# An attention and mixer kernel on one core: q and k of the last four batches loaded in token order and turned by DMA transposes

## The chip, the core and the metric

The kernel runs on one NeuronCore of a Trainium2 chip. The core has a matmul engine (TensorE, PE; its weight loads are listed as PEld), a vector engine (VectorE, DVE), an activation engine (ScalarE, ACT), a general engine (GpSimd, POOL) and a synchronising engine (SyncE, SP). DMAs are issued from queues: here SP's and POOL's, and ACT's once at the start. They all move their data through the core's 16 DMA engines. The metric is the device time of one execution in microseconds.

## The reference

The reference computes causal attention in which 16 extra "beacon" keys and values stand ahead of each batch's own, and then a mixer in two steps.

```python
# q, k, v: [B=8, H=8, S=576, D=64]; beacon_k, beacon_v: [8, 8, 16, 64]
k_all = concatenate([beacon_k, k], axis=2);  v_all = concatenate([beacon_v, v], axis=2)
scores = q @ k_all.T / sqrt(D);  scores[causal] = -1e9       # beacons are seen by every query
x = softmax(scores) @ v_all                                   # to [8, 576, 512]
u = x + (x.T @ U @ V).T                                       # rank 32, over the 576 tokens
out = u + relu(u @ w_ch1) @ w_ch2                             # 512 -> 2048 -> 512, float32
```

## The kernel before, in words

The inputs are float32. All products run in float16 and add up in float32 in PSUM, which is handed out as eight banks in turn.

**Attention.** The work goes by pairs of heads: 8 batches with 4 pairs each, p = 0 to 31, with `b, c = divmod(p, 4)`. Scores are made with keys on partitions, so both q and k are needed with channels on partitions (`qT`, `kT`). For a pair, `regroup_of` (L483, the copy itself at L218, on DVE) reorders the loaded q and k into `pr`. `qkT_units` (L221) then turns them on PE, in one unit for q and one for k: one transpose of the first 80 rows (L227) and four of 128 columns (L229). DVE brings each result out of PSUM in two copies (L230, L231). `score_units` (L238) makes the scores (L257) in two visits, has ACT exponentiate them (L263), and DVE applies the masks (L244, L246). `av_unit` (L277) multiplies with v (L281) and divides by the sums (L289, L290) into `xb`. A pair's scores are made one pair ahead of its products with v, and its transposes two pairs ahead.

**Loads.** POOL's queue casts to float16 on the way. For q and k it makes pieces of four neighbouring tokens a partition and head (`main_load`, L167) and a small load of the first tokens (`head_load`, L161); beacons have their own (L164). v comes in token order, 128 tokens a tile, in five DMAs (L174). The tiles of q and k alternate between two buffers, and so do `kT` and v. Batch 0's q and k come in float32 through SP and ACT and are rounded on chip by ACT, DVE and POOL (`group_first`, L477).

**Mixer.** `mix_units` (L294) adds the low-rank term to a batch's x and stores it turned in `uT`. Its head is one unit, its parts are six. Where it is "turned", five DMA transposes on SP's queue (L301) bring x to `uT`, and DVE adds the term in place (L341). Otherwise PE transposes x (L325) and adds the term in PSUM, and ACT (L345) or DVE (L343) copies it out. `mlp_units` (L351) makes blocks of 512 rows: 16 units of the first product with a relu (g, L370, relu on ACT L374 or DVE L376) and 16 units of the second (c, L386). Each unit is four matmuls of 512 columns; every fourth c unit ends in an addition on DVE (L399) and an output store on SP (L404), from four buffers. A block begins with four DMA transposes on SP (L360).

**Order.** The order of all engines is written out by hand. Mixer and MLP units wait in a queue, and `fill` takes a number of them, the quota, between the parts of a pair's attention. `mix` (L546) is called for a batch when its last pair is done. It takes the turned form if the batch is 2 or later and the queue holds at least 17 units (`LAG + 5`), and then puts the head behind 12 of them. Batches 0 and 1 run with the counts in `FIRST`; then come 16 units, and seven more among the attention of the next pairs; from batch 2 on the quota applies. What is left in the queue runs at the end.

```python
turned = b >= NF and len(queue) >= LAG + 5                   # L548
quota = 8 if b == NF else 9 if c == 0 else 8                 # L655, NF = 2
```

Of the kernel before, what the change touches and what calls it, by code (L numbers as in the profile page):

```python
# [17 lines left out]
P = 128  # L18
# [9 lines left out]
def kernel(  # L28
# [57 lines left out]
    loads = ctx.enter_context(tc.tile_pool(name="loads", bufs=2))  # L86
# [96 lines left out]
    def qk_tiles():  # L183

        hd = [loads.tile([P, H, D], F16, name=f"hd{i}", tag=f"hd{i}") for i in range(2)]
        st = [stage.tile([P, H, 4 * D], F16, name=f"st{i}", tag=f"st{i}") for i in range(2)]
        return hd, st
# [9 lines left out]
    def emit_loads(b, L, vs):  # L197
        k_loads(b, L, ALLH)
        q_loads(b, L, ALLH)
        beacon_load(nc.gpsimd, beacon_k[b], L[0][0], ALLH)  # L200
        v_loads(v[b], beacon_v[b], vs, ALLH)
# [237 lines left out]
    def load_batch(b):  # L439
        Ls[b] = qk_tiles()  # L440
        emit_loads(b, Ls[b], vss[b % 2])
# [5 lines left out]
    def load_first():  # L447
# [4 lines left out]
        hd = [loads.tile([P, H, D], F16, name=f"hd{i}", tag=f"hd{i}") for i in range(2)]  # L452
        Ls[0] = hd, [main[:, i, :, :] for i in range(2)]
# [47 lines left out]
    def qkT_of(p):  # L501
        b, c = divmod(p, NH2)
        new_qT_of(p)
        return qkT_units(Ls[b], prs[p], qTs[b], kTs[b % 2], c)
# [15 lines left out]
    AHEAD = 16  # L520
    LAG = 12
# [3 lines left out]

    IDLE = [10, 3, 2, 2]
    queue = []
    state = {"t": 0}

# [32 lines left out]
    with tc.manual_schedule(engines={ENG.PE, ENG.Activation, ENG.DVE, ENG.SP, ENG.Pool}):  # L562
# [41 lines left out]
        for p in range(NP1):  # L604
# [8 lines left out]
            if p + 2 < NP1:  # L613
                if p == 0:
                    seq.append(lambda: group_first(2, 1, V))
                elif p == 1:
                    seq.insert(1, lambda: group_first(3, 1, act_copy))
                else:
                    seq.append(lambda p=p: regroup_of(p + 2))
                qk = [lambda i=i, p=p: qkT_of(p + 2)[i]() for i in range(2)]  # L620
            seq += av[0:1] + qk + av[1:2]
            if p + 2 < NP1:
                new_qT_of(p + 2)
                sc = scores_of(p + 2)
                seq.append(lambda sc=sc, p=p: sc[0](IDLE[3] if p < NH2 else 0))
# [16 lines left out]
        for p in range(NP1, NP):  # L642
            b, c = divmod(p, NH2)
            if c == 0 and b + 1 < B:
                load_batch(b + 1)
            sc = scores_of(p + 1) if p + 1 < NP else []
            qk = []
            if p + 2 < NP:
                regroup_of(p + 2)
                qk = qkT_of(p + 2)  # L650
            av = av_of(p)
# [3 lines left out]
            quota = 8 if b == NF else 9 if c == 0 else 8  # L655
# [112 lines left out]
```

## Time and profile before

| | before |
|---|---|
| median of 3 runs | 377.83 us (377.72 to 378.54) |
| profiled execution | 378.74 us, its span 377.1 us |
| busy PE, DVE, ACT, POOL | 360.0, 217.9, 170.3, 85.6 us |
| DMA | 100349 packets, 36.33 MB |
| POOL's queue (q0) | 65904 packets, 17.54 MB, 49.9% of 16 engines' span |
| SP's queue (q1) | 33952 packets, 17.90 MB, 19.8% |

In the profile's lines, L12 is line 12 of the kernel before. A group of instructions stands as `output<-inputs`, with tile sizes as partitions x elements. After the bar come the busy time in us, the mean of one in ns, and the time the engine was idle just ahead of these instructions, with what ended it. In a timeline a row has its start, its length in us (of all its instructions together), engine and line, and in brackets the idle time ahead of it. A "q" behind an engine's name is its queue of DMAs; the length there is that of issuing, not of moving the data. The DMA share of a stretch is the time of all packets over the time of 16 engines; packets overlap on an engine, so it can be over 1.

### The profile page before, as it was taken

To read this page: it belongs to the slowest core of one execution; us is meant where nothing else is said; L and a number is where in the kernel's file an instruction comes from. 1 tells how busy PE (TensorE), PEld (TensorE's weight loads), DVE (VectorE), ACT (ScalarE), POOL (GpSimd) and SP (SyncE) were. 2 spreads that over 40 slices of the span, in tenths; PEclk is the share of its full clock that TensorE was granted. 3 is DMA by queue.
4 is the path that set the end of the run, shared out by engine and by line. 5 is a ranking of instruction groups with operands and counts; after the bars stand their busy time and mean duration, and the time that the engine had idled before them with its cause. 6 is when DMAs were issued, how large, how long until landed. Compare 5 with 4: busy or idle time off the path is not lost.

```text
span 377.1 us, 7980 instructions
## 1 busy us (share of the span) xinstructions
PE 360.0 (95%) x3180; PEld 185.4 (49%) x3180; DVE 217.9 (58%) x602; ACT 170.3 (45%) x370; POOL 85.6 (23%) x126
## 2 busy tenths in 40 slices
PE   6768999999999999989999999989999999999995
PEld 2546455454555554544465545544554444444442
DVE  5868763465658666665666675785677352222311
ACT  3758662466435653466445663467441301401300
POOL 9998537302105302230323050000000000000000
PEclk9889999999999999999999999999999999999999
DMA  9999999944719951995199799133012402103111
GB/s 181 205 146 206 194 197 136 195 105 58 101 57 106 117 56 59 93 152 62 13 111 132 111 53 105 56 85 57 9 58 85 91 30 97 42 30 108 33 49 72
DMA packets 100349, 36.33 MB, mean 96 GB/s; under 512 B 76112, under 2 KB 94544, under 8 KB 100304
## 3 DMA queue, kind: packets, MB, share of 16 engines
q0 software_dynamic: 65904, 17.54, 49.9%
q1 hardware_dynamic: 33952, 17.90, 19.8%
q8 instruction: 27, 0.44, 0.5%
q10 hardware_dynamic: 448, 0.30, 0.3%
q14 instruction: 18, 0.15, 0.1%
HBM read 37.86 MB, written 9.44 MB: 125 GB/s over the span
## 4 chain that ended last, share of the span: by engine, by line
PE 89%; DVE 6%; ACT 2%; DMA 1%; SPq 1%; issue 1%; ACTq 0%
PE gps L370 34%; PE cps L386 33%; PE sps L257 7%; PE po L281 7%; PE tps L229 3%; PE ups L335 2%; ACT expt L263 1%; PE ups L325 1%; DMA stm<-in_q_dram 1%; DVE kT L231 1%; PE qtp L310 1%; DVE qT L231 1%; DVE xb L290 1%; PE tps L227 1%; DVE expt L244 1%
## 5 line engine op out<-in xcount | busy, mean ns | idle before, releaser
L263 ACT ACTIVATE expt<-sps 128x496 f16<-128x496 f32 (+2 forms) x256 | 111.2, 531 | 82.3 <-PE sps L257 82.3
L370 PE MATMUL gps<-uT,w 128*128 128x512 f16 x576 | 137.8, 379 | 1.2 <-ACT uT L345 1.2
L386 PE MATMUL cps<-w,gT 128*128 128x512 f16 x576 | 137.8, 379 | 0.0
L374 ACT ACTIVATE gT<-gps 128x512 f16<-128x512 f32 x86 | 51.5, 606 | 93.1 <-PE gps L370 91.9
L386 PEld LDWEIGHTS <-gT 128*128 128x128 f16 x576 | 52.4, 98 | 56.4 <-issue 4.4
L370 PEld LDWEIGHTS <-w 128*128 128x128 f16 x576 | 51.4, 97 | 57.2 <-issue 5.1
L376 DVE TENSOR_SCALAR gT<-gps 128x512 f16<-128x512 f32 x58 | 39.9, 690 | 41.4 <-PE gps L370 39.7
L399 DVE TENSOR_TENSOR ob<-cps,ut 128x512 f32<-128x512 f32 x32 | 22.1, 690 | 42.8 <-PE cps L386 42.2
L281 PEld LDWEIGHTS <-expt 128*128 128x128 f16 (+1 forms) x960 | 38.2, 99 | 12.4 <-DVE expt L246 0.7
L174 POOL DMA_DIRECT2D vs<-in_v_dram x50 | 40.1, 815 | 13.8 <-DMA w<-in_moe_w_ch_dram 6.0
L281 PE MATMUL po<-vs,expt 128*128 128x65 f16 (+1 forms) x960 | 40.8, 195 | 0.5 <-DVE expt L244 0.2
L257 PE MATMUL sps<-qT,kT 64*128 64x80 f16 (+4 forms) x384 | 34.3, 291 | 4.4 <-DVE kT L231 4.3
L244 DVE TENSOR_TENSOR expt<-expt,bigmask 128x512 f16<-128x512 f16 x64 | 27.0, 422 | 12.6 <-ACT expt L263 12.2
L290 DVE TENSOR_TENSOR xb<-po,rec 128x320 f16<-128x320 f32 x64 | 31.4, 491 | 2.2
L289 DVE RECIPROCAL rec<-po 128x5 f32<-128x5 f32 x64 | 12.0, 188 | 27.9 <-PE po L281 27.7
L257 PEld LDWEIGHTS <-kT 64*128 64x128 f16 x384 | 12.5, 96 | 31.2 <-issue 14.2
L229 PE MATMUL tps<-ident,pr 128*128 128x128 f16 x256 | 24.6, 222 | 0.5 <-DVE pr L218 0.5
L231 DVE COPY qT<-tps 128x512 f16<-128x512 f16 x32 | 21.8, 680 | 0.0
L231 DVE COPY kT<-tps 128x512 f16<-128x512 f16 x32 | 21.7, 678 | 0.0
L164 POOL DMA_DIRECT2D vs<-in_beacon_v_dram x10 | 5.3, 535 | 70.1 <-PE po L281 69.9
L229 PEld LDWEIGHTS <-pr 128*128 128x128 f16 x256 | 16.3, 99 | 6.2 <-DVE pr L218 0.8
L227 PE MATMUL tps<-ident,hd 80*128 80x80 f16 x64 | 13.1, 204 | 4.1 <-ACT hd L473 2.9
(65 smaller groups left out, 185.3 us busy)
## 6 DMA issues: line engine op xcount, KB each, us to landing
out_dram<-ob SPq DMA_DIRECT2D x36, 256.0 KB, 2.2
w<-in_moe_w_ch_dram POOLq DMA_DIRECT2D x4, 1024.0 KB, 11.5
st<-in_k_dram POOLq DMA_DIRECT2D x6, 512.0 KB, 6.9
st<-in_q_dram POOLq DMA_DIRECT2D x6, 512.0 KB, 7.5
vs<-in_v_dram POOLq DMA_DIRECT2D x18, 128.0 KB, 6.6
stm<-in_k_dram SPq DMA_DIRECT2D x4, 256.0 KB, 4.5
vs<-in_v_dram POOLq DMA_DIRECT2D x12, 64.0 KB, 6.5
stm<-in_q_dram SPq DMA_DIRECT2D x3, 256.0 KB, 5.9
```

The costliest lines, as they stand in the source:

```text
L174: nc.gpsimd.dma_start(out=dst[a : a + nq[j], j, :, :], in_=src[hs, ds(q0[j], nq[j]), :].rearrange("h p d -> p h d"))
L229: nc.tensor.transpose(ps[:, ds(NL + P * j, P)], pr[i][:, j, :, :], ident)
L231: nc.vector.tensor_copy(out=dst[:, c, w - 4 * P : w].rearrange("x (p j) -> x p j", j=4), in_=ps[:, NL:SK].rearrange("x (j p) -> x p j", j=4),)
L244: nc.vector.tensor_tensor(out=e4, in0=e4, in1=bigmask, op=ALU.min)
L257: nc.tensor.matmul(ps[g, i][:, ds(o, w)], kT[hp, c, ds(P * ch, P)], qT[hp, c, ds(qa, w)], start=True, stop=True,)
L263: nc.scalar.activation(out=ex[i][:, ds(SLOT * g, gw[g])], in_=ps[g, i][:, 0 : gw[g]], func=AF.Exp, scale=scale)
L281: nc.tensor.matmul(po[:, j, :], ex[0 : nk[c], ds(blk[(c, j)], P)], vs[0 : nk[c], ds(c * H * E + h * E, E)], start=(c == 0), stop=(c == j),)
L290: nc.vector.tensor_tensor(out=xb[:, :, ds(h * D, D)], in0=po[:, :, 0:D], in1=r.broadcast_to([P, NT, D]), op=ALU.mult)
L370: nc.tensor.matmul(g[:, 0:n], w1[:, cc, ts(dc, P)], uT[:, cc, ds(t0, n)], start=(cc == 0), stop=(cc == NCC - 1))
L374: nc.scalar.activation(out=gT["t"][:, dc, 0:n], in_=g[:, 0:n], func=AF.Relu)
L376: nc.vector.tensor_scalar_max(out=gT["t"][:, dc, 0:n], in0=g[:, 0:n], scalar1=0.0)
L386: nc.tensor.matmul(ps[:m, :], gT["t"][:, dc, ds(P * i, m)], w2[:, dc, :], start=(dc == 0), stop=turned and dc == NDC - 1, skip_group_check ...
```

## The change

It has four parts.

1. For batches 4 to 7 (`DT0 = 4`) q and k are loaded in token order: five DMAs each for q and k, 128 tokens a tile as v has them, and one for the beacons (`load_whole`). They are issued at the third pair of the batch two before. v's loads stay where they were.
2. Those tiles are turned by ten DMA transposes a batch on SP's queue (`turns`), straight into `kT` and `qT`: four ahead of each of the first two pairs of the batch before, and two ahead of the third. `regroup_of` and `qkT_of` are no longer called for pairs of batches 4 to 7.
3. The rounding of the last q set of batch 0 (`group_first(3, 1, act_copy)`) moves from the second pair, behind its exponentials, to the end of the first pair, ahead of the next scores.
4. The quota is 4 in batch 2 and 9 in all later pairs.

The tiles for the first tokens (`hd`) now lie in the same tile as the others (`st`), so both come free together.

```diff
-    loads = ctx.enter_context(tc.tile_pool(name="loads", bufs=2))
...
     def qk_tiles():
-        hd = [loads.tile([P, H, D], F16, name=f"hd{i}", tag=f"hd{i}") for i in range(2)]
-        st = [stage.tile([P, H, 4 * D], F16, name=f"st{i}", tag=f"st{i}") for i in range(2)]
-        return hd, st
+        t = [stage.tile([P, NT * DM], F16, name=f"st{i}", tag=f"st{i}") for i in range(2)]
+        st = [x[:, 0 : 4 * DM].rearrange("p (h e) -> p h e", h=H) for x in t]
+        hd = [x[:, 4 * DM :].rearrange("p (h d) -> p h d", h=H) for x in t]
+        whole = [x[:, :].rearrange("p (j h d) -> p j h d", h=H, d=D) for x in t]
+        return hd, st, whole
...
     def load_batch(b):
+        if b < DT0:
+            Ls[b] = qk_tiles()
+            emit_loads(b, Ls[b], vss[b % 2])
+        else:
+            v_loads(v[b], beacon_v[b], vss[b % 2], ALLH)
+
+    def load_whole(b):
         Ls[b] = qk_tiles()
-        emit_loads(b, Ls[b], vss[b % 2])
+        for i, (src, m) in enumerate(((k[b], nk), (q[b], nq))):
+            dst = Ls[b][2][i]
+            if i == 0:
+                beacon_load(nc.gpsimd, beacon_k[b], dst[:, 0, :, :], ALLH)
+            for j in range(NT):
+                a = m[j] - nq[j]
+                nc.gpsimd.dma_start(
+                    out=dst[a : m[j], j, :, :], in_=src[:, ds(q0[j], nq[j]), :].rearrange("h p d -> p h d")
+                )
+
+    def turns(b):
+        new_qT(b)
+        kn, qn = Ls[b][2]
+        us = []
+        for j in range(NT):
+            for n, dst, o, m in ((kn, kTs[b % 2], P * j, nk[j]), (qn, qTs[b], q0[j], nq[j])):
+                us.append(
+                    lambda n=n, dst=dst, o=o, m=m, j=j: nc.sync.dma_start_transpose(
+                        out=dst[:, :, ds(o, m)], in_=n[:m, j, :, :].rearrange("p h d -> p (h d)")
+                    )
+                )
+        return us
...
-        Ls[0] = hd, [main[:, i, :, :] for i in range(2)]
+        Ls[0] = qk_tiles()[0], [main[:, i, :, :] for i in range(2)]
...
+    DT0 = 4
+    QUOTA = {2: 4}
+    def fill_turns(tr, n):
+        for u in tr[:n]:
+            u()
+        del tr[:n]
...
                 if p == 0:
                     seq.append(lambda: group_first(2, 1, V))
-                elif p == 1:
-                    seq.insert(1, lambda: group_first(3, 1, act_copy))
-                else:
+                elif p > 1:
                     seq.append(lambda p=p: regroup_of(p + 2))
...
                 sc = scores_of(p + 2)
+                if p == 0:
+                    seq.append(lambda: group_first(3, 1, act_copy))
...
             if c == 0 and b + 1 < B:
                 load_batch(b + 1)
+            if c == 2 and DT0 <= b + 2 < B:
+                load_whole(b + 2)
+            if c == 0 and DT0 <= b + 1 < B:
+                tr = turns(b + 1)
...
-            if p + 2 < NP:
+            if p + 2 < min(NP, DT0 * NH2):
                 regroup_of(p + 2)
                 qk = qkT_of(p + 2)
+            if DT0 <= b + 1 < B and c < 3:
+                fill_turns(tr, 4)
...
-            quota = 8 if b == NF else 9 if c == 0 else 8
+            quota = QUOTA.get(b, 9)
```

More of the change, by code (lines that the diff above doesn't have):

```diff
@@ L451, in load_first @@
         raw["head"] = head
-        hd = [loads.tile([P, H, D], F16, name=f"hd{i}", tag=f"hd{i}") for i in range(2)]
-        Ls[0] = hd, [main[:, i, :, :] for i in range(2)]
+        Ls[0] = qk_tiles()[0], [main[:, i, :, :] for i in range(2)]
         def kload(hs):
```

## The prediction

> **What bounds the kernel now.** I read the first two parts of the page, then a table of stretches (one row for each batch), then the chain of waits in order of time, then single pairs of heads on the timeline.
>
> ```profile
> span 377.1 us, 7980 instructions
> PE 360.0 (95%) x3180; PEld 185.4 (49%) x3180; DVE 217.9 (58%) x602; ACT 170.3 (45%) x370; POOL 85.6 (23%) x126
> PE   6768999999999999989999999989999999999995
> ```
>
> The last row is PE's busy share in 40 slices of 9.4 us: from the fifth on it is nearly everywhere nine tenths or more. Busy alone proves little, as matmul records overlap, so the next rows look at start-to-start times. In the table of stretches the columns are length, busy time of PE, PEld, DVE, ACT, POOL, clock, DMA share, GB/s. The 65 to 75 row lies before batch 2, the next two are batches 2 and 3, the last is a stretch of the tail.
>
> ```profile
> 65.00:75.00 10.00, 9.97 (x71) 4.85 (x70) 3.50 (x9) 4.00 (x9) 4.07 (x5) 1.00 1.77 187
> 75.00:113.00 38.00, 38.00 (x344) 19.44 (x343) 23.10 (x67) 19.98 (x44) 3.68 (x5) 1.00 0.48 82
> 113.00:148.80 35.80, 35.80 (x362) 18.91 (x361) 24.96 (x70) 20.17 (x45) 8.47 (x12) 1.00 0.82 81
> 289.00:302.00 13.00, 13.00 (x80) 5.84 (x78) 7.07 (x17) 4.78 (x8) 0.00 (x0) 1.00 0.46 106
> ...
> 287.98 12.09 PE gps L370 x56
> ```
>
> In the tail 56 matmuls of 512 columns take 12.09 us: 216 ns each, with nothing between them. One unit of the MLP queue is four of these, 0.864 us. Now one pair of heads in batch 5, on PE alone:
>
> ```profile
> 203.31 0.58 PE L257 MATMUL sps<-qT,kT 64*128 64x496 f16 x4
> ...
> 209.38 0.20 PE L227 MATMUL tps<-ident,hd 80*128 80x80 f16 x1
> 209.42 0.39 PE L229 MATMUL tps<-ident,pr 128*128 128x128 f16 x4
> 209.64 1.03 PE L370 MATMUL gps<-uT,w 128*128 128x512 f16 x4
> ...
> 212.79 0.38 PE L257 MATMUL sps<-qT,kT 64*128 64x496 f16 x2
> ```
>
> A pair lasts 212.79 - 203.31 = 9.48 us with eight units (8 x 0.864 = 6.91), so its attention costs PE 2.57 us, and no gap is left. From the fifth slice on, about 40 us, the time is PE's work; whatever is taken from PE's stream there comes off the end, as far as nothing else becomes late.
>
> The Trainium skill (Trainium Kernel Development and Optimization, Performance Expectations) calls matmul busy time a bad metric and points to weight-load busy time, here 49%. By it PE would have slack and a removal would give less; the 216 ns spacing disagrees, and I keep the rule as rival B.
>
> **The change, part by part.**
>
> *Transposes on PE.* For batches 4 to 7 the calls that transpose q and k on PE fall away: 4 batches x 4 pairs x 2 = 32 units of one 80-column and four 128-column transposes.
>
> ```profile
> L227 PE MATMUL tps<-ident,hd 80*128 80x80 f16 x64 | 13.1, 204 | 4.1 <-ACT hd L473 2.9 <-DVE hd L481 1.2
> ```
>
> 64 such units exist, 32 go. By start-to-start time a unit costs 209.64 - 209.38 = 0.26 us (not the 0.59 us of overlapping records): 32 x 0.26 = **8.3 us off PE**. The regrouping copies (L218) and the evacuations (L230, L231) leave DVE with them; DVE is not the bound, so that saves nothing by itself, except a stall on kT in batch 6 where the DVE was behind:
>
> ```profile
> 248.20 0.58 PE L257 MATMUL sps<-qT,kT 64*128 64x496 f16 x4 [1.20 <-DVE kT L231]
> ```
>
> That wait has nothing to wait for any more: **1.2 off**.
>
> *The quotas.* I counted the unit queue through the loops. It holds 32 units when batch 2 begins. Before, quotas 8,8,8,8 and then 9,8,8,8 leave 0, 6, 12, 18, 24 and 30 at the ends of batches 2 to 7. After, 4 a pair and then 9 leave 16, 19, 22, 25, 28 and 31. So the tail keeps its size (101 units, then 102), but a mix is taken as "turned" (its x by DMA, not by PE) when the queue holds at least 17: before for batches 5, 6 and 7, after for 3 and 4 too; batch 2 misses it by one unit. Each turned mix saves 20 PE transposes:
>
> ```profile
> L325 PE MATMUL ups<-ident,xb 128*128 128x128 f16 x60 | 8.8, 220 | 0.0
> ...
> 115.99 0.38 PE L325 MATMUL ups<-ident,xb 112*128 112x112 f16 x4
> ...
> 116.21 0.37 PE L335 MATMUL ups<-Vsb,qts 128*128 128x240 f16 x2
> ```
>
> 60 is 12 in each of five unturned batches, which confirms the count. Four take 0.22 us, so 20 take 1.05 (a little more for the wide, less for the narrow): **2.1 off** for two batches. It puts ten more transposes on SP and six additions in place of six copies a batch; DVE has 11 of 36 us free there. One wait stays:
>
> ```profile
> 164.50 0.38 PE L370 MATMUL gps<-uT,w 128*128 128x512 f16 x1 [1.16 <-ACT uT L345]
> ```
>
> Here the sixth and last part of batch 3's mix stood one unit ahead of the first unit that reads it. By the count it does so again in batch 4's third pair, on DVE instead of ACT: equal, 0.
>
> *A thin batch 2.* With 16 units fewer, batch 2's PE work shrinks from 38 to 38 - 16 x 0.864 = 24.2 us. It still holds all 16 g units, so ACT keeps its 19.98, and DVE keeps 23.10 less four of these output additions, 20.3:
>
> ```profile
> L399 DVE TENSOR_TENSOR ob<-cps,ut 128x512 f32<-128x512 f32 x32 | 22.1, 690 | 42.8 <-PE cps L386 42.2
> ```
>
> PE remains longest by 3.9 us. The other bound: with no units between them the pairs of batch 0 follow each other at chain length,
>
> ```profile
> 11.83 1.50 PE L257 MATMUL sps<-qT,kT 64*128 64x496 f16 x12 [0.89 <-DVE kT L231]
> ...
> 16.48 0.88 PE L257 MATMUL sps<-qT,kT 64*128 64x496 f16 x12 [0.23 <-DVE kT L231]
> ```
>
> 4.65 us each. Were none of that covered by the four units, a pair would take 4.65 + 3.46 = 8.11 instead of 2.57 + 3.46 = 6.03: 4 x 2.08 = 8.3 us. Between 0 and +8.3 I take **+0.8**, near the low end, since the batch row shows every engine below PE.
>
> *The moved rounding.* The copies of the first batch's last q set on ACT move from behind pair 2's exponentials to ahead of them.
>
> ```profile
> 15.36 0.41 ACT L263 ACTIVATE expt<-sps 128x208 f16<-128x208 f32 x1
> 16.89 3.38 ACT L263 ACTIVATE expt<-sps 128x496 f16<-128x496 f32 x8 [1.13 <-PE sps L257]
> 20.09 0.70 ACT L473 ACTIVATE pr<-stm 128x512 f16<-128x512 f32 x1
> 20.61 0.34 ACT L473 ACTIVATE hd<-sth 80x128 f16<-80x128 f32 x1
> ...
> 21.00 0.21 PE L227 MATMUL tps<-ident,hd 80*128 80x80 f16 x1 [2.86 <-ACT hd L473]
> ```
>
> PE waits 2.86 us for them. ACT idles 1.13 us before 16.89, about what both copies take (1.04). Their data is there just in time, by the rows of the tile of first rows:
>
> ```profile
> L161 SPq DMA_DIRECT2D sth<-in_q_dram x1: 418/418/418, 9.2 to 9.2; - x1
> ...
> DMA to landing us min/median/max: 6.4/6.4/6.4
> ```
>
> 9.2 + 6.4 = 15.6, ACT is free at 15.77. But what PE gains runs into batch 1's v:
>
> ```profile
> L174 POOL DMA_DIRECT2D vs<-in_v_dram x2: 679/724/770, 24.4 to 25.2; - x2
> ...
> DMA to landing us min/median/max: 2.7/2.9/3.0
> ...
> 28.85 0.84 PE L281 MATMUL po<-vs,expt 128*128 128x65 f16 x13 [0.22 <-DVE expt L244]
> ```
>
> It lands at 25.2 + 2.7 = 27.9, and its first product starts at 28.85 today: about 0.95 us can be kept there. From -1 (data late, the exponentials wait) to 2.9 I take **1.0 off**.
>
> *What is added.* POOL issues 11 DMAs a batch where it had 5; SP issues 10 transposes a batch.
>
> ```profile
> 149.29 4.21 POOL L174 DMA_DIRECT2D vs<-in_v_dram  x5
> ...
> 148.80:157.60 8.80, 8.80 (x97) 4.69 (x95) 5.14 (x17) 3.49 (x8) 4.69 (x6) 1.00 1.30 131
> 160.80:174.60 13.80, 12.56 (x118) 6.50 (x115) 7.96 (x24) 10.34 (x25) 3.69 (x5) 1.00 1.12 146
> ...
> 207.80 5.71 SPq L360 DMA_TRANSPOSE ut<-uT  x4
> 221.41 7.51 SPq L301 DMA_TRANSPOSE uT<-xb  x5
> ...
> L301 SPq DMA_TRANSPOSE uT<-xb x5: 1251/1301/2174, 221.4 to 227.7; - x5
> DMA to landing us min/median/max: 4.3/5.6/6.4
> ...
> 241.10 0.66 DVE L341 TENSOR_TENSOR uT<-ups,uT 128x480 f16<-128x480 f32 x1
> ```
>
> The new loads have the shape of v's, twice: issue 2 x 4.21 plus a beacon, 9 us on an idle POOL. Batch 4's start when pair 11's transposes have freed the tile, late in batch 2's second pair, and have two pairs (12 us) before SP's turns are called, five before the first scores. SP had nothing else queued in batch 2, and between 213.5 and 221.4 it stood idle, so the four turns of a batch's first pair run ahead of that pair. They stand before the mix's own five transposes (7.51 us, 1.5 each); the last of those was issued at 227.7, landed 4.3 us later at 232.0, and the first addition that needs them began at 241.1. Even if four turns, 6 us, stood wholly in front, they fit into these 9 us. Later turns delay output stores at most; with four buffers, one filled every four units (4.7 us), that is covered for over 10 us, and past it a stalled DVE addition would hold PSUM and so PE. I put **+0.5** for what is not seen, between 0 and +12 (rival C).
>
> **The sum**: -8.3 - 1.2 - 2.1 + 0.8 - 1.0 + 0.5 = -11.3 us. The profiled execution took 378.74 (span 377.1 and 1.6 around it), 0.9 above the median of 377.83; 367.4 by the one, **366.5 by the other**, which I forecast.
>
> **The rivals.**
>
> *A, batch 2 starves PE.* For it: DVE and ACT would have to work 83% of the time (20 of 24.2 us), and in the rows of batches 2 and 3 neither works over 70%. Against it: in those rows PE waits for neither. At half the upper bound, 4.2 in place of 0.8: 366.5 + 3.4 = **370**.
>
> *B, the freed time does not come out*, because ACT, DVE and the order of units pace the batches. Then only the kT wait, the start and a part of the mixes are gained, about 3: **375**. For it speaks that records overlap, so that 95% busy is no proof; the tail's 216 ns and the pair without a gap speak against.
>
> *C, SP's queue is held by the turns (slower).* If loads are late at a batch's first pair, SP stands at a turn, and the mix's five transposes stand behind it. Their additions (L341) then wait in DVE's order, ahead of reciprocals and evacuations, and PE stops. Loads become late if the DMA engines saturate. One batch of v is 1.30 x 8.8 = 11.4 us of DMA time, q and k now 1.12 x 13.8 - 4 x 0.65 = 12.9, in the new order 22.8; a transpose is at most 0.46 x 13 / 9 = 0.65, as nine are issued in the stretch from 289 to 302. So a batch goes from 0.82 x 35.8 = 29.4 to 29.4 + 9.9 + 6.5 + 3.3 = 49 us of DMA time in 37.5: a share of 1.31, where 1.77 was held from 65 to 75 us. The margin left in front of the additions is 9 - 6 = 3 us; from 3 + 11.3 / 3 = 6.8 us of lateness in each of batches 4, 5 and 6 on the change loses. At 8 us: 366.5 + 15 = **381.5**.
> The Trainium skill (DMA: Bandwidth & Descriptors, Specifications) gives 512 B as the least piece at line rate, smaller ones being read, modified and written; pieces drop from 512 to 128 B here. The 22.8 against 12.9 us agrees in direction; how much of it is that mechanism no run here shows.
>
> *D, the start gives all of its 2.86 us*: **364.6**. The wait's own row speaks for it, the landing of batch 1's v at 27.9 against. *E, batches 3 and 4 are not turned after all*, since a few units miss in the count: **368.6**. For it, that batch 2 misses by one; against, that the count gives the 60 records.
>
> **How the numbers follow.** Forecast (364 to 369) 0.62, A 0.12, B 0.07, C 0.08, D 0.08, E 0.03. Time 366.5. The range takes in the low bounds (-8.3 - 1.2 - 2.1 - 2.9 - 1.2 for the wait at 164.5 = -15.7, 362) and A with some more of the upper ones, 373.5; B's centre and C are out. A measurement of this kernel tells 0.2% from no change. Faster is all but C and half of B (whose loss would be total): 0.88; same 0.04; slower 0.08.
>
> **What would show it.** Transposes on PE: 32 records on the 80-column line, and pairs in batches 4 to 7 of nine units in 2.05 + 7.78 = 9.8 us. Quotas: 36 wide mix transposes (three batches of 12) in place of 60. Batch 2: pairs of 6 us; over 7 is A. Start: no 2.86 us wait, the first product with batch 1's v at about 28. SP: additions L341 that never idle on a DMA; idle DVE ahead of them is C. Wrong above all would be PE gaps over 1 us after 100 us.

## The result and the profile after

| | before | after |
|---|---|---|
| median, side by side on one chip | 378.14 us (377.72 to 378.54, 4 runs) | 365.93 us (365.40 to 366.37, 4 runs) |
| profiled execution, its span | 378.74, 377.1 us | 365.4, 363.7 us |
| DMA packets, MB | 100349, 36.33 | 149692, 42.21 |

The ratio is 0.9676, with a 95% interval of 0.9660 to 0.9692: the change takes 12.2 us off. In a second comparison the unaltered changed kernel (f0_after below) had 0.9697 (0.9666 to 0.9728).

These are the first parts of the page of the kernel after, and the two DMA queues from its third part (packets, MB, share of 16 engines). In this kernel's lines the code stands one line further down around the attention (L257 is now L258, L370 is L371, L386 is L387), and the turns are L468.

```profile
span 363.7 us, 7602 instructions
PE 348.0 (96%) x2980; PEld 174.6 (48%) x2980; DVE 190.1 (52%) x514; ACT 167.5 (46%) x362; POOL 105.8 (29%) x150
PE   6778999999999999979999999999999999999995
q0 software_dynamic: 90352, 17.47, 64.0%
q1 hardware_dynamic: 58848, 23.87, 34.2%
```

PE is still the busy one from about 40 us on, with one notch: the seven further on, at 155 to 164 us. The two hundred instructions that left PE are the 160 transposes of q and k and the 40 of two mixes. POOL's queue moves the same megabytes as before (17.54) in 90352 packets where it had 65904, and its packets take 64.0% of the engines' time where they took 49.9%.

The table of stretches of the kernel after (length, busy time of PE, PEld, DVE, ACT, POOL, clock, DMA share, GB/s): batch 2, batch 3, and two stretches of the next batches. Below it stand two rows of PE's timeline, the first scores of two neighbouring pairs with nine units between them, and then the last row of matmuls in the chain of waits.

```profile
74.60:98.80 24.20, 24.20 (x276) 13.13 (x274) 18.80 (x60) 19.36 (x43) 9.52 (x13) 1.00 1.29 116
98.80:135.50 36.70, 36.70 (x353) 19.02 (x352) 21.28 (x59) 19.19 (x43) 14.47 (x19) 1.00 1.27 129
135.50:172.70 37.20, 35.19 (x315) 17.00 (x316) 17.88 (x47) 18.91 (x41) 13.69 (x18) 1.00 1.52 141
172.70:207.40 34.70, 34.70 (x313) 16.88 (x312) 19.69 (x50) 17.22 (x38) 13.56 (x18) 1.00 1.46 135
```

```profile
125.69 0.58 PE L258 MATMUL sps<-qT,kT 64*128 64x496 f16 x4
...
135.52 0.58 PE L258 MATMUL sps<-qT,kT 64*128 64x496 f16 x4
```

```profile
345.51 13.83 PE cps L387 x64
```

Batch 2 lasts the predicted 24.2 us with PE busy throughout, a pair of nine units 135.52 - 125.69 = 9.83 us, and the tail's matmuls are still 13.83 / 64 = 0.216 us apart. The third stretch has a hole of 2.0 us in PE. This is what lies in it, on PE and on SP's queue:

```profile
160.41 0.38 PE L371 MATMUL gps<-uT,w 128*128 128x512 f16 x1 [0.46 <-DVE uT L342]
161.45 0.38 PE L371 MATMUL gps<-uT,w 128*128 128x512 f16 x1 [0.66 <-DVE uT L342]
...
163.03 0.37 PE L258 MATMUL sps<-qT,kT 64*128 64x464 f16 x2 [0.89 <-DMA qT<-st]
```

```profile
153.77 1.23 SPq L468 DMA_TRANSPOSE kT<-st  x1
155.09 1.75 SPq L468 DMA_TRANSPOSE qT<-st  x1
159.97 0.34 SPq L405 DMA_DIRECT2D out_dram<-ob  x1
```

The first two waits are the mix of batch 3, whose last part comes just ahead of its first reader (1.12 us; 1.16 before, on ACT), in batch 4's third pair as forecast. The third is new: the first scores of batch 5, which were due at 161.8, wait for that batch's last two turns, which SP issued at 153.8 and 155.1.

Where the time went, by the start of first scores on PE (the marks are the same pairs in both traces; pair 7 is the last of batch 1, pair 9 the second of batch 2):

| | before | after | difference |
|---|---|---|---|
| start to pair 7 | 46.41 | 44.35 | -2.06 |
| pair 7 to pair 9 | 30.26 | 30.26 | 0 |
| pair 9 to PE's end | 295.88 | 284.71 | -11.17 |
| of it, PE busy | 293.44 | 282.69 | -10.75 |
| of it, PE idle | 2.44 | 2.02 | -0.42 |
| PE's end to the end of the span | 4.52 | 4.42 | -0.10 |

### The profile page after: what moved, and what is told of

Same layout as the page of the kernel before. It is cut to its first block, busy times and chain, and to the rows that moved or that the text cites. A ratio compares the mean times of both kernels' runs of the same rounds, so it can differ in the third digit from the quotient of the medians.

```text
span 363.7 us, 7602 instructions
## 1 busy us (share of the span) xinstructions
PE 348.0 (96%) x2980; PEld 174.6 (48%) x2980; DVE 190.1 (52%) x514; ACT 167.5 (46%) x362; POOL 105.8 (29%) x150
## 2 busy tenths in 40 slices
DMA packets 149692, 42.21 MB, mean 116 GB/s; under 512 B 133649, under 2 KB 143889, under 8 KB 149649
## 3 DMA queue, kind: packets, MB, share of 16 engines
q0 software_dynamic: 90352, 17.47, 64.0%
## 4 chain that ended last, share of the span: by engine, by line
PE 81%; DMA 15%; POOL 2%; SPq 1%; issue 1%; DVE 0%; POOLq 0%
PE gps L371 33%; PE cps L387 31%; PE po L282 6%; PE sps L258 6%; DMA st<-in_k_dram 3%; DMA w<-in_moe_w_ch_dram 2%; DMA vs<-in_v_dram 2%; DMA qT<-st 2%; DMA stm<-in_k_dram 2%; DMA st<-in_q_dram 2%; PE ups L336 2%; PE tps L230 1%; POOL vs L173 1%; DMA stm<-in_q_dram 1%; PE qtp L311 1%; PE ups L326 1%
## 5 line engine op out<-in xcount | busy, mean ns | idle before, releaser
L371 PE MATMUL gps<-uT,w 128*128 128x512 f16 x576 | 135.3, 379 | 1.6 <-DVE uT L342 1.1
L387 PE MATMUL cps<-w,gT 128*128 128x512 f16 x576 | 135.8, 379 | 0.0
L371 PEld LDWEIGHTS <-w 128*128 128x128 f16 x576 | 52.3, 98 | 60.6 <-issue 4.1
L387 PEld LDWEIGHTS <-gT 128*128 128x128 f16 x576 | 52.9, 98 | 58.4 <-issue 3.0
L258 PE MATMUL sps<-qT,kT 64*128 64x80 f16 (+4 forms) x384 | 33.8, 286 | 4.3 <-DVE kT L232 3.4
L258 PEld LDWEIGHTS <-kT 64*128 64x128 f16 x384 | 12.5, 95 | 31.5 <-issue 15.8
L342 DVE TENSOR_TENSOR uT<-ups,uT 128x336 f16<-128x336 f32 (+1 forms) x30 | 16.6, 553 | 6.5 <-PE ups L336 6.4
L456 POOL DMA_DIRECT2D st<-in_q_dram x20 | 16.8, 873 | 3.3 <-DMA uT<-xb 3.0
L456 POOL DMA_DIRECT2D st<-in_k_dram x20 | 16.9, 867 | 2.8 <-DMA vs<-in_v_dram 2.8
L336 PE MATMUL ups<-Vsb,qts 128*128 128x240 f16 (+1 forms) x64 | 15.7, 286 | 0.0
L247 DVE TENSOR_TENSOR expt<-expt,mask 80x80 f16<-80x80 f16 x64 | 12.5, 196 | 0.0
```

The costliest lines, as they stand in the source:

```text
L258: nc.tensor.matmul(ps[g, i][:, ds(o, w)], kT[hp, c, ds(P * ch, P)], qT[hp, c, ds(qa, w)], start=True, stop=True,)
L336: nc.tensor.matmul(ups[:, i, :], cell["q"], Vsb[:, cc, ds(a, n)], start=first and i == 0, stop=True, skip_group_check=True,)
L371: nc.tensor.matmul(g[:, 0:n], w1[:, cc, ts(dc, P)], uT[:, cc, ds(t0, n)], start=(cc == 0), stop=(cc == NCC - 1))
L387: nc.tensor.matmul(ps[:m, :], gT["t"][:, dc, ds(P * i, m)], w2[:, dc, :], start=(dc == 0), stop=turned and dc == NDC - 1, skip_group_check ...
L456: nc.gpsimd.dma_start(out=dst[a : m[j], j, :, :], in_=src[:, ds(q0[j], nq[j]), :].rearrange("h p d -> p h d"))
```

## The experiments

Each kernel is named by its label. Its ratio is to the kernel before, run beside it on the same chip, with a 95% interval. The kernels came in three groups, each on one chip: e1_round, e2_quota, e3_turns and e4_pe_back (before: 378.01 us); e6_early, e7_twice, e8_dt3 and e11_turns_first (378.86); f0_after, e5_dve_back, e10_unturned and e9_early_q3 (377.56). Where a kernel is compared with the kernel after, the difference is given by the ratios, or by the traces from pair 9 to PE's end.

### e1_round: the moved rounding alone

```diff
 # on the kernel before
-                elif p == 1:
-                    seq.insert(1, lambda: group_first(3, 1, act_copy))
-                else:
+                elif p > 1:
...
+                if p == 0:
+                    seq.append(lambda: group_first(3, 1, act_copy))
```

> The kernel before with the moved rounding alone (group_first(3, 1) on ACT ahead of pair 2's exponentials). Theory: PE's stream sets the end from about 35 us on, so what the start gains stays gained. After the change the first scores of pair 7 stood 2.06 us earlier (44.35 against 46.41): 2.1 us faster than before. The prediction's term was 1.0, rival D 2.86; a loss at the end of what the start gained (the start was never on the path) would give 0.

Measured: 376.27 us, 0.9953 (0.9932 to 0.9974), so 1.7 us off (1.0 to 2.6). In its trace pair 7's first scores start at 43.66 (46.41 before), and from pair 9 to PE's end it takes 295.88 us, to the hundredth what before takes. What the start gains is kept. More than a wait went away there. The stretches of 18 to 26 us, first of the kernel before, then of the kernel after; the third column from the end is the granted clock:

```profile
18.00:22.00 4.00, 1.14 (x31) 1.01 (x27) 1.21 (x4) 2.95 (x8) 3.47 (x6) 1.00 1.56 183
22.00:26.00 4.00, 3.85 (x46) 2.22 (x43) 3.25 (x13) 2.35 (x6) 3.73 (x6) 0.57 1.69 154
```

```profile
18.00:22.00 4.00, 3.37 (x64) 2.31 (x61) 3.68 (x15) 3.51 (x10) 3.59 (x6) 1.00 1.48 182
22.00:26.00 4.00, 2.65 (x47) 1.73 (x43) 3.26 (x12) 2.68 (x8) 2.84 (x4) 1.00 1.52 149
```

Before, PE worked 1.14 of 4 us around the 2.86 us wait, and the clock granted in the next 4 us was 0.57. After, it works 3.37 us and the clock stays at 1.00. It does so in e1_round too, while e2_quota, e3_turns and e11_turns_first, which keep the old place of the rounding, show 0.77, 0.57 and 0.77 there.

### e2_quota: the quotas alone

```diff
 # on the kernel before
-            quota = 8 if b == NF else 9 if c == 0 else 8
+            quota = 4 if b == NF else 9
```

> The kernel before with the new quotas alone (4 in batch 2, then 9); q and k are still transposed by PE everywhere. Theory: two more mixes are turned, 2 x 1.05 = 2.1 us off PE, and the thin batch 2 costs nothing (its pairs 6.03 us apart): 2.1 us faster, less any new wait. Rival A: batch 2 starves, 3.4 us slower than that, so 1.3 slower than before.

Measured: 374.37 us, 0.9887 (0.9863 to 0.9910), 3.6 us off. Batch 2, with its transposes still on PE:

```profile
76.11 0.58 PE L257 MATMUL sps<-qT,kT 64*128 64x496 f16 x4
...
82.20 0.58 PE L257 MATMUL sps<-qT,kT 64*128 64x496 f16 x4
```

```profile
L325 PE MATMUL ups<-ident,xb 128*128 128x128 f16 x36 | 5.3, 219 | 0.0
```

A pair is 6.09 us, the same as in the kernel after: the thin batch costs nothing at a quota of four. 36 wide transposes are left of 60, so two mixes more are turned, as counted. From pair 9 to PE's end it is 292.36, or 3.52 less than before: PE's busy time is 290.80, 2.64 less, where the mixes were counted at 2.1, and its idle time is 0.9 less. The wait of 1.20 us on kT in batch 6 is gone in this kernel too, though DVE still evacuates every transpose, while the mix's own wait is longer (1.56 us on DVE in place of 1.16 on ACT). So the order of the units alone is enough to remove the wait on kT.

### e3_turns: loads and turns alone

```diff
 # on the kernel after
-                elif p > 1:
+                elif p == 1:
+                    seq.insert(1, lambda: group_first(3, 1, act_copy))
+                else:
...
-                if p == 0:
-                    seq.append(lambda: group_first(3, 1, act_copy))
...
-            quota = QUOTA.get(b, 9)
+            quota = 8 if b == NF else 9 if c == 0 else 8
```

> The new loads and DMA transposes alone, with the old quotas and the rounding in its old place. Theory: 32 units of 0.26 us less on PE and the kT wait of 1.2 gone, 9.5 us faster, less up to 1.2 where turns land late for a batch's first scores. Rival B (other engines pace the batches): under 4 us faster.

Measured: 375.15 us, 0.9915 (0.9883 to 0.9947), 2.9 us off where 9.5 were forecast, and with a wide spread: its executions ran from 371.89 us, at a mean granted clock of 0.999, to 379.69, at 0.981. The last is the profiled one, so its trace shows where the time can go, at its largest. In the list of waits (total, times, longest; PEld's row is the same stall as the shorter of PE's two, 2.42 us):

```profile
PE sps L258 <- DMA qT<-st: 6.4, 2, 4.0
PEld L258 <- DMA kT<-st: 2.7, 1, 2.7
```

In each, first scores wait for late turns. The larger one, on PE, and SP's queue ahead of it:

```profile
180.04 0.57 PE L258 MATMUL sps<-qT,kT 64*128 64x464 f16 x2 [3.99 <-DMA qT<-st]
```

```profile
162.34 1.97 SPq L468 DMA_TRANSPOSE kT<-st  x1
164.40 1.43 SPq L468 DMA_TRANSPOSE qT<-st  x1
165.93 6.06 SPq L361 DMA_TRANSPOSE ut<-uT  x4
172.08 1.20 SPq L468 DMA_TRANSPOSE kT<-st  x1
173.37 1.20 SPq L468 DMA_TRANSPOSE qT<-st  x1
```

The last two turns of batch 5 are called for the third pair, and by then a block of the MLP has put its four transposes into the queue; they take 6.06 us of it. The turns are issued at 172.1 and 173.4 and land at 179.6 and 179.9. PE stands for 4 us, and then a second loss follows:

```profile
175.60:180.00 4.40, 0.45 (x3) 0.10 (x2) 0.69 (x1) 0.58 (x1) 0.00 (x0) 0.90 1.15 64
180.00:186.00 6.00, 5.96 (x29) 2.61 (x29) 1.38 (x3) 2.08 (x4) 0.00 (x0) 0.50 0.00 0
186.00:190.00 4.00, 4.00 (x38) 2.01 (x37) 1.58 (x6) 2.02 (x5) 0.00 (x0) 1.00 0.01 2
```

For 6 us behind the wait the granted clock is 0.50. That pair takes 15.95 us where its neighbour in the trace takes 8.96: 7.0 us, 4.0 of waiting and 3.0 of half speed.
The Trainium skill (TensorE: Matmul & The Clock Gate, Why this matters for your kernels) says to leave PE no idle gaps of more than about 3 us, since one idle window puts the clock back to half. The traces agree as far as they go: waits of 3.45 us (e8_dt3) and 3.99 us were followed by 0.50, one of 2.04 us (e9_early_q3) by 1.00. The 2.86 us at the start of the kernel before, with little work around it, were followed by 0.57 (e1_round above).

### e11_turns_first: the same, with the turns as 5, 5, 0

```diff
 # on e3_turns
-                fill_turns(tr, 4)
+                fill_turns(tr, 5)
```

> As the run with the loads and turns alone (old quotas, rounding in its old place), but the ten turns of a batch stand 5 and 5 ahead of its predecessor's first two pairs, none ahead of the third. Theory: that run lost its gain because the last two turns stood on SP behind a block's four transposes and landed at 179.9 us, 4 to 7 us after the first scores that need them; in front of those four they land in time and the gain of 9.5 us comes out, 368.5. Rival (the DMA engines are too full, whatever the order on SP): it stays at about 375.

Measured: 369.89 us, 0.9781 (0.9742 to 0.9820), 8.3 us off. One digit brings back 5 us of e3_turns' missing gain. All ten turns now stand ahead of the block's transposes:

```profile
165.72 1.24 SPq L468 DMA_TRANSPOSE qT<-st  x1
167.05 6.00 SPq L361 DMA_TRANSPOSE ut<-uT  x4
```

From pair 9 to PE's end it is 287.90, or 7.98 less than before; PE's busy time is 285.51, 7.93 less. One wait for a turn is left in it, at batch 6's first scores:

```profile
209.32 0.37 PE L258 MATMUL sps<-qT,kT 64*128 64x464 f16 x2 [0.69 <-DMA qT<-st]
```

The wait on kT is gone here too, with the old order of units, so either change removes it. So the transposes are worth about 8 us on PE, and it was the turns' place in SP's queue, not the loads or the transposes' own cost, that kept e3_turns from them.

### e4_pe_back: PE's time given back

```diff
 # on the kernel after; two matmuls of 512 columns a pair, for the pairs of batches 4 to 7
+            if sc and p + 1 >= DT0 * NH2:
+                sc = [lambda s0=sc[0]: s0(2)] + sc[1:]
```

> The changed kernel with two matmuls of 512 columns that compute nothing ahead of each pair's scores in batches 4 to 7: 16 x 2 x 0.216 = 6.9 us of PE work given back, nothing else. Theory (PE's stream sets the time): 6.9 us slower than the changed kernel, about 5.3 us faster than the kernel before. Rival B (PE has slack there): no more than 1 us slower than the changed kernel.

Measured: 370.20 us, 0.9797 (0.9770 to 0.9823), 3.8 to 4.6 us more than the kernel after by the two ratios of that one. From pair 9 to PE's end it is 290.39, 5.68 more than after, for 6.9 us of work put in. Most of the 1.2 between is the wait of batch 5's first scores (1.07 by the length of that pair), which the list of waits no longer has: with pairs of 10.26 us the late turn is in time. PE's stream sets the time of these batches.

### e6_early: the changed kernel with its turns as 5, 5, 0

```diff
 # on the kernel after
-                fill_turns(tr, 4)
+                fill_turns(tr, 5)
```

> The changed kernel with the turns 5, 5 and 0 in place of 4, 4 and 2. Theory: the wait of batch 5's first scores for a turn (0.9 and some 0.3 us at 161.8 to 163.0) goes, so 1.0 to 1.3 us faster than the changed kernel, a ratio to before of about 0.964. Rival: the turns now push back the mixes' own transposes and additions wait on DVE, no gain or a loss of some us.

Measured: 362.94 us (362.52 to 363.59), 0.9585 (0.9559 to 0.9610): faster than the kernel after (0.9676 and 0.9697), with intervals that don't touch, and the fastest of all. On SP's queue the place where the two late turns stood has a store:

```profile
150.54 1.26 SPq L468 DMA_TRANSPOSE qT<-st  x1
151.89 7.86 SPq L405 DMA_DIRECT2D out_dram<-ob  x3
159.80 5.16 SPq L361 DMA_TRANSPOSE ut<-uT  x4
```

No first scores wait any more, the pair that took 10.90 us (161.76 to 172.66) takes 9.83, and pair 9 to PE's end is 283.49, 1.22 less than after. The medians differ by more (3.4 us by the first ratio, 4.2 by the second). The executions of this kernel had mean granted clocks of 0.997 to 1.000, those of f0_after 0.990 to 0.999; the two of f0_after at 0.999 took 364.0 and 364.9 us. Whether the late turns lower the clock in some of them no trace shows: f0_after's profiled execution was its best, and that of the kernel after (0.994) has its one lowered stretch at the start (0.58 from 11 to 14 us), before any turn. The clock also varies without turns (0.993 to 1.000 in e1_round). So 1.2 us is what the traces show for the new order, and the rest of the medians' difference stays open.

### e7_twice: the turns of batches 5 to 7 made twice

```diff
 # on the kernel after; the second copy goes to a tile that nobody reads
+                if b > DT0:
+                    us.append(
+                        lambda n=n, m=m, j=j: nc.sync.dma_start_transpose(
+                            out=pairs.tile([P, 4, 2, D], F16, name=f"pr{j % 2}", tag=f"pr{j % 2}").rearrange(
+                                "p a b d -> p a (b d)"
+                            )[:, :, 0:m],
+                            in_=n[:m, j, :, :].rearrange("p h d -> p (h d)"),
+                        )
+                    )
...
-                fill_turns(tr, 4)
+                fill_turns(tr, 8 if b + 1 > DT0 else 4)
```

> The changed kernel with every turn of batches 5, 6 and 7 made twice, the second time into a tile that nobody reads: 30 more DMA transposes, 1.3 us each on SP, 10 a batch. Rival C of the prediction, put to the test: the margin on SP's queue is small, so turns land later by up to 13 us a batch and first scores or additions wait, 10 to 30 us slower than the changed kernel. The prediction's own view (margin of 3 us in front of the mix's additions and a whole pair in front of the first scores): 0 to 6 us slower.

Measured: 396.02 us, 1.0455 (1.0421 to 1.0488): 29 us more than the kernel after by either ratio, at the upper end of what rival C expected and far outside the 0 to 6 of the prediction's own view. The waits for turns:

```profile
PE sps L258 <- DMA qT<-st: 24.5, 6, 5.2
```

Six waits of 24.5 us in all, at the first scores of batches 5, 6 and 7, and the clock behind them again at half (0.50 from 165.5 to 173). From pair 9 to PE's end it is 316.81, 32.1 more than after: 23.6 of it is idle time of PE, and the other 8.5 is the same work at a lower clock. No row names an addition (L342) that waits for a DMA. So SP's queue can turn this change into a loss, as rival C had it, but at another place.

### e8_dt3: the turns from batch 3 on

```diff
 # on the kernel after
-    DT0 = 4
+    DT0 = 3
...
+                if b + 1 == DT0:
+                    load_whole(b + 1)
```

> The changed kernel with batch 3 loaded in token order and turned by DMA as well (its loads ahead of its v, as soon as the tile is free). Theory: 8 more units off PE, 8 x 0.26 = 2.1 us faster than the changed kernel, 363.8. Rival: from 60 to 75 us the DMA engines are full, batch 3's pieces of 128 B land late and SP stands at them, 0 to 5 us slower.

Measured: 369.17 us, 0.9736 (0.9706 to 0.9767), 2.3 us slower than the kernel after by its first ratio and 1.5 by its second, whose interval overlaps. Batch 3's first scores wait for its last turns. These are the two rows of PE, and two of SP's queue:

```profile
94.73 0.60 PE L258 MATMUL sps<-qT,kT 64*128 64x496 f16 x2 [3.45 <-DMA qT<-st]
97.24 0.57 PE L258 MATMUL sps<-qT,kT 64*128 64x464 f16 x2 [1.92 <-DMA qT<-st]
```

```profile
81.70 6.44 SPq L361 DMA_TRANSPOSE ut<-uT  x4
...
94.77 1.20 SPq L468 DMA_TRANSPOSE qT<-st  x1
```

The rival has the outcome, but not the reason. The loads were there: they were issued by 69 us and landed in 6 us or less, SP's list of waits has no turn of batch 3 that waits for one, and the turns landed in 2.3 to 5.0 us. SP came to the first turn only at 74.8, behind output stores, and six of the ten stood behind a block's four transposes; the last was issued at 94.8, when its scores were already due. The clock is 0.50 from 94.7 to 99 us. The transposes that are saved don't pay for that in this order of SP's queue; another order, such as 5, 5, 0, was not run with it.

### f0_after, the kernel after once more, and e5_dve_back: DVE's time given back

> The changed kernel once more, unaltered, so that the next three stand beside it on one chip. Ratio to before 0.966 to 0.970.

Measured: 366.29 us (364.00 to 367.68), 0.9697 (0.9666 to 0.9728).

```diff
 # on the kernel after; five DVE operations a pair, for the pairs of batches 4 to 7, which nobody reads
+            if p + 2 < NP and not qk:
+                def busy(n, i):
+                    for _ in range(n):
+                        t = pairs.tile([P, 4, 2, D], F16, name=f"pr{i}", tag=f"pr{i}")
+                        nc.vector.tensor_tensor(...)
+                qk = [lambda: busy(3, 0), lambda: busy(2, 1)]
```

> The changed kernel with five DVE operations of 0.42 us that nobody reads in each pair of batches 4 to 7, at the places of the copies that the change removed (2.1 us a pair, 29 us in all). Theory: DVE is not the bound, the copies that fell away saved nothing by themselves: within 1 us of the changed kernel. Rival: part of the gain is DVE's relief, 3 us or more slower.

Measured: 365.97 us, 0.9690 (0.9663 to 0.9717), no different from f0_after beside it. DVE's busy time rises from 190.0 to 215.5 us, near the 217.9 of before, and nothing follows; from pair 9 to PE's end it is 284.23, against 284.93 in f0_after. The relief of DVE is worth nothing by itself, as the prediction had it.

### e10_unturned: batches 3 and 4 not turned

```diff
 # on the kernel after
-        turned = b >= NF and len(queue) >= LAG + 5
+        turned = b >= 5 and len(queue) >= LAG + 5
```

> The changed kernel with the mixes of batches 3 and 4 not turned, as before (PE transposes x for them): 40 PE transposes back. By the prediction's term 2.1 us slower than the changed kernel. If ten DMA transposes less relieve SP enough, part of it comes back (0.9 to 1.2 us, the late turn of batch 5): only 1 us slower.

Measured: 364.71 us (364.13 to 365.11), 0.9655 (0.9628 to 0.9682). Giving back the 2.1 us of the mixes should have cost 2.1; it costs nothing, and the middle is 1.6 us on the faster side of f0_after, with overlapping intervals. PE's wide mix transposes are 60 again:

```profile
L326 PE MATMUL ups<-ident,xb 128*128 128x128 f16 x60 | 8.8, 220 | 0.0
```

But neither the wait for the mix of batch 3 nor that for batch 5's turns is in this trace (1.12 and 1.07 us in the kernel after), and PE has no gap at all from pair 9 to its end: 284.13 us against 284.71. With five transposes fewer on SP in each of two batches the turns come in time. The last two are issued hardly earlier (8.6 us ahead of their first scores, 8.0 in the kernel after), but they land in 4.9 and 3.9 us in place of 8.4 and 7.8: the loads are over sooner, with a DMA share of 0.23 from 156 to 160 us where the kernel after has 1.89 and more from 155 to 163. And a mix that isn't turned starts behind 2 units of the queue in place of 12, so that its last part is done well ahead of its first reader (146.5 and 159.5 us here). The two turned mixes take 1.4 to 1.8 us off PE's busy time (282.4 to 282.7 in the traces of the kernel after, f0_after, e5_dve_back and e6_early, 284.13 here), and give it back as these two waits. e6_early, with the turned mixes and no late turns, is 0.64 shorter than this kernel; that order without the turned mixes was not run.

### e9_early_q3: e6_early with a quota of three in batch 2

```diff
 # on e6_early
-    QUOTA = {2: 4}
+    QUOTA = {2: 3}
```

> The changed kernel with the turns 5, 5, 0 and a quota of 3 in batch 2. 20 units are then left when batch 2 ends, so its mix is turned too (1.05 us off PE), and batch 4's mix no longer ends one unit ahead of the first that reads it (up to 1.4 us). Theory: 2 us faster than the 5, 5, 0 order alone, 361; batch 2's pairs 5.2 us apart. Rival A: now batch 2 starves, pairs over 5.7 us, no gain or slower.

Measured: 370.87 us, 0.9815 (0.9777 to 0.9853), some 8.7 us slower than e6_early by the ratios. First scores of batch 2's pairs, and its stretch:

```profile
81.48 0.58 PE L258 MATMUL sps<-qT,kT 64*128 64x496 f16 x4 [1.16 <-DVE kT L232]
...
87.05 0.58 PE L258 MATMUL sps<-qT,kT 64*128 64x496 f16 x4 [0.31 <-DVE kT L232]
```

```profile
75.00:98.50 23.50, 21.25 (x259) 11.36 (x256) 18.00 (x58) 18.55 (x41) 9.83 (x13) 1.00 1.38 116
```

A pair with three units has 2.57 + 3 x 0.864 = 5.16 us of work on PE. They take 6.39, 5.57, 5.68 and 5.82: 2.8 us of starving in the batch. The rest lies behind it. Turns are late again: a block's four transposes stand ahead of a batch's turns in both kernels, but with the queue shifted by four units SP issues them at 125.5, 167.1 and 207.5 us in place of 122.5, 159.8 and 199.8, and the turns behind them come later too. First scores wait for turns at four places (5.7 us in all), one of them here:

```profile
199.34 0.70 PE L258 MATMUL sps<-qT,kT 64*128 64x496 f16 x4 [2.04 <-DMA qT<-st]
...
199.40:206.00 6.60, 6.60 (x51) 3.08 (x52) 2.44 (x7) 3.49 (x8) 0.00 (x0) 1.00 0.24 92
```

The first row is of the timeline, the second of the table of stretches: behind this wait the clock stays at 1.00.

From pair 9 to PE's end it is 291.09, 7.6 more than e6_early.

## Why the prediction was right, and where it was not

366.5 us was forecast for a median of 365.93. The sum was -11.3; the medians side by side differ by 12.2, the two spans (377.07 and 363.74) by 13.3. The direction and the main term held. Of the 2.0 us by which the spans differ more, 1.1 is the start and 0.8 the thin batch, which cost nothing. That the time came within 0.6 us is partly luck: the sum missed by 0.9 us on the medians and by 2.0 on the spans, and it started from 377.83, where the run side by side had 378.14.

**Transposes on PE, -8.3.** Right. 32 calls are gone, nine-unit pairs take 9.83 us as forecast (9.8), e11_turns_first gains 8.0 with 0.7 us of a late turn still in it, and 6.9 us of other work put in their place cost 5.7 (e4_pe_back). The rule of the Trainium skill (Trainium Kernel Development and Optimization, Performance Expectations) that was kept as rival B takes weight-load busy time, 48% here, as the better metric. Read as slack on PE it would have made e4_pe_back nearly free; that run speaks against this reading for this kernel.

**The kT wait, -1.2.** The size is right, it is the row's own. The reason is half of it: without the evacuations the wait is gone in the old order of units as well (e3_turns, e11_turns_first), but e2_quota loses it with all of them in place. Two parts of the change remove it, and it counts once.

**The mixes, -2.1.** The count is right (36 records), and the saving on PE's work is about right (2.6 us in e2_quota, 1.4 to 1.8 by e10_unturned). That it comes off the end is wrong in the changed kernel: e10_unturned is no slower without it. In e2_quota, with no turns on SP, it does come off. Two steps failed. One put ten more transposes on SP at no cost; with them batch 5's last turns land late, 1.07 us. The other took the mix's wait as one that stays either way ("equal, 0"): with quotas of nine a mix that isn't turned has no such wait, so 1.12 us of it are the turned form's price.

**The thin batch, +0.8.** It cost nothing; pairs of 6.03 to 6.09 us against 6.03 of work. The bound of 8.11 a pair had a real mechanism, PE waiting for kT, which begins one unit lower (e9_early_q3). The forecast sat one step from an edge and didn't know it.

**The moved rounding, -1.0.** This is the term that was mis-sized: the start gave 2.06 us in the compared traces. In the ten traces with the moved rounding pair 7's first scores start at 42.5 to 44.8 us, with a mean of 43.57, and in the four without at 45.9 to 46.8, with a mean of 46.36: 2.8 between the means. By the medians of e1_round it is 1.7. The limit that the prediction set was the landing of batch 1's v at 27.9 "and its first product starts at 28.85". That row's product belongs to batch 0's last pair; batch 1's come in the next pair, in the trace after at 31.89:

```profile
31.89 0.63 PE L282 MATMUL po<-vs,expt 128*128 128x65 f16 x15
```

There the last of v's five loads was issued at 26.1 and had landed by 29.5, so v was some 2 us early. In the kernel after PE waits instead for batch 1's q and the first weights of the MLP, for which it didn't wait before:

```profile
23.11 0.21 PE L228 MATMUL tps<-ident,st 80*128 80x80 f16 x1 [0.87 <-DMA st<-in_q_dram]
...
35.62 1.04 PE L371 MATMUL gps<-uT,w 128*128 128x512 f16 x4 [0.50 <-DMA w<-in_moe_w_ch_dram]
```

The prediction also left out that the wait was followed by a lowered clock, which went with it. The measured 1.7 to 2.8 lies between the term and rival D's 2.86, from the wait's own row.

**What is added, +0.5.** About the right size: 1.1 us of late turns. The reasoning failed in "Later turns delay output stores at most". It looks at what stands behind the turns in SP's queue; what mattered was when they are called, what stands ahead of them, how long they take to land, and who reads them. In the kernel after the last two were issued 8 us ahead of the first scores and took 8 us to land; in e3_turns a block's four transposes stood ahead of them. And the margin was reckoned at the mix's additions (9 us there, 6 needed), where only e9_early_q3 shows a wait for a DMA (2.2 us). At the first scores of batch 5 there was no margin. "The four turns of a batch's first pair run ahead of that pair" held for three batches of four: they were issued from 89.3, 129.2 and 165.7 us, and the pairs begin at 98.8, 135.5 and 172.7. Batch 7's stood behind a block's transposes and were issued from 206.9, as their pair began at 207.4. For batch 4 SP stood at its loads, the longest waits of these lines of its queue:

```profile
SPq L468 <- DMA st<-in_k_dram: 9.1, 3, 6.6
SPq L468 <- DMA st<-in_q_dram: 4.5, 1, 4.5
```

Nothing else was queued there, so that did no harm.

**The rivals.** A is false at four units and true at three. B is false (e4_pe_back). C's mechanism is real in part (e7_twice, e3_turns, e8_dt3): turns held on SP do make PE wait. But first scores wait in place of additions, and C left out the clock behind the waits: 3.0 us beside a wait of 3.99 in e3_turns, 8.5 beside 23.6 us of idle time in e7_twice. The DMA share that it reckoned, 1.31, was nearly met or passed (1.27, 1.52, 1.46), and it was borne. E is false by the records.

**The sum.** From pair 9 to PE's end PE's busy time fell by 10.75 us, where the two terms for it make 10.4. Its idle time fell by 0.42: the wait on kT (1.20) went, and 0.89 came for the late turn. With -2.06 at the start and -0.10 behind PE's end that is the -13.3 between the two spans; 0.4 us of it is in no term.

## What to carry to other kernels

When work moves from an engine to a queue, take each transfer that is moved and ask three things: what stands ahead of it in that queue when it is called, how long it takes to land under that stage's load and not alone, and which instruction reads it first. Gains of parts don't add when the parts share a queue and the DMA engines: here a saving of some 2 us of PE's work was worth nothing, half because with its transposes others landed late and half because its own last part came just ahead of its reader. An order of 5, 5, 0 in place of 4, 4, 2 took 1.2 us back, and 5 us in the kernel with the old quotas. A long wait of PE is to be priced with the clock behind it.

## What the runs showed of the hardware that was not expected

**A long wait can be paid twice.** Behind waits of 3.45 and 3.99 us the granted clock was 0.50 for some 6 us, and 3 us of work were lost in e3_turns beside the wait. Even the 2.86 us wait at the start of the kernel before, in a stretch where PE had little to do anyway, was followed by 0.57. A wait of 2.04 us in the midst of full work left it at 1.00.

**The landing of a DMA transpose goes with the load of the DMA engines.** All 40 turns of the kernel after, from issue to landing:

```profile
DMA to landing us min/median/max: 2.3/4.8/10.0
```

Take for each turn the DMA share of the 8 us behind its issue. The 14 turns with a share under 0.9 landed in 2.3 to 4.5 us, the 18 with 1.7 or more in 5.1 to 10.0, and the 8 between in 2.5 to 6.5. The late ones, issued at 153.8 and 155.1, had shares of 1.88 and 1.93 and took 8.4 and 7.8 us; the last two, at 227.1 and 228.4 with the loads done, took 2.3. Issuing one took SP 1.2 us in the median, and up to 2.7.

**Loads in token order took more of the DMA engines' time for the same bytes.** POOL's queue took 64.0% in place of 49.9% of the engines' time for 17.5 MB, in pieces of 128 B for the last four batches' q and k; by the spans that is 233 us in place of 188. The number of transposes beside it doesn't move it: it is 230 us in e7_twice with 30 more of them and 242 in e10_unturned with ten fewer, and 233 and 242 in the two traces of the kernel after. That the pieces are the reason is what is left, and no run shows it by itself.
